# An S4D mixer with a channel MLP: kernel tables through DRAM, table products on GpSimd, outer products as blocks of their own

## The chip, the core and the metric

The kernel runs on one core of a Trainium2 chip. The metric is the device time of one execution in microseconds (us), median of three runs. The engines are TensorE (PE; its weight loads are shown apart as PEld), VectorE (DVE), ScalarE (ACT), GpSimd (POOL) and SyncE (SP, which issues most transfers).

## What is computed

The reference, cut to what matters (L = 2048 tokens, D = 576 channels, N = 128 states, F = 4608):

```python
xn = layernorm(A_u)
# s: a long convolution per channel, whose kernel K is made from the parameters
dt = exp(log_dt);  A = -exp(log_A_real) + 1j * A_imag;  C = (C_real + 1j * C_imag) * dt
P = exp((A * dt)[:, :, None] * arange(L))          # D x N x L
K = 2 * einsum("dn,dnl->dl", C, P).real
s = causal_conv(xn, K) + xn * D_skip               # by FFT
# g: an MLP over the channels of each token
h = gelu(layernorm(xn) @ w1 + b1)
g = silu(h @ w2 + b2)
out = A_u + s * g
```

## The kernel before

**The MLP is the frame.** 48 slots run one after the other: 12 groups of 384 hidden units, twice (two halves of the tokens), for two blocks of 512 tokens each. A slot is three products of layer 1 (line 633; 14 matmuls into a bank `mxa` or `mxb`, float32 split into a high and a low part, so that each product is done three times) and eight pieces of layer 2 (line 707; 72 matmuls of 288 columns). Between the two stand, for each of the three products, a GELU (ACT, 671), its high part `hh` (ACT, 674) and its low part `hl` (DVE, 677). DVE adds layer 2 to `acc` (717). ACT and DVE also split each weight tile, `raw`, into two parts (586, 583). Where the program finds it possible, the small last matmuls of two layer-1 products of the next slot are done ahead as a pair of half-height matmuls (`pair`, line 616); the two products then have 13 matmuls and not 14.

**The convolution is laid between.** The convolution kernel is made from 36 tables of 16 channels (`tables`, from line 953). For a table, `load_par` (944) fetches 16 channels' parameters from DRAM to `par` on POOL's queue; DVE multiplies angle and time into a phase (963, `w<-par,tv`) and adds a start (966); ACT and DVE cut it to its fraction and fold it (969, 972, 975), ACT takes two sines (980, 982); DVE multiplies powers into magnitudes `mg` (988, two instructions) and weighs the sines with them (997 to 1003). Then `kgen` does the outer products on PE (line 1042), a block of 64 small matmuls into a bank `cv`, and ACT copies it to `kt` in SBUF (1047). Six chunks of 96 channels (`chunk`, from line 1076) take these, with `xn`, through an FFT made of matmuls: 12 blocks `x1` (1157), 12 blocks `k1` (1188), 24 blocks `s2` (1217), 12 inverse blocks (1260) and 6 blocks `i1` (1286), with copies, transposes and products on ACT and DVE between them.

**What sets the order.** A planner (class `Order`) writes the order of each engine's instructions. It keeps a clock for each engine from fixed costs (`dve(n)`, `act(n)`, `pool(n)`), takes the steps of each line of work when its clock says that what they need is ready, and pins the result: each engine runs its instructions in that order. Steps of GELU and `hl` are urgent; others are put where they fit in ahead of these by the planner's clock. A block of the convolution is placed on PE when the planner's clock says that its input has been ready for 0.4 us (`pe_turns`, 1584). For the outer products there are two ways. `ride` (1053) puts them into another convolution block, so that PE goes from the MLP to both and back once. Otherwise `pe_turns` places them alone, after a patience `ALONE` of 20 us and not ahead of a date `DUE`. `HOLD` (1074) puts eight single steps behind the next instruction or two of their engine.

In DRAM stand among others `par_s` (the parameters of all channels), `xn_s`, `s_s` (the convolution's result), and `f2q`, `g2p` (the FFT's matrices, loaded as `f2t` and `g2t` on SP's queue, 1097 and 1100).

Of the kernel before, what the change touches and what calls it, by code (L numbers as in the profile page):

```python
# [28 lines left out]
E1, E8, E64, E512 = 2, 10, 18, 26  # L29
NPAR = 30  # L30
PK = 144
NXC, NROW = 1, 4
# [15 lines left out]
def pool(n):  # L48
    return 0.25 + 0.0023 * n

# [174 lines left out]
def mixer_kernel(ctx, tc, u, log_a_real, a_imag, c_real, c_imag, log_dt, d_skip, w1, b1, w2, b2,  # L225
# [24 lines left out]
    par_s = dr.tile([P, D, NPAR], F32, name="par_s")  # L250

# [13 lines left out]
    f1t = sb.tile([P, 2, 2, 64], F32, name="f1t")  # L265
# [34 lines left out]
    def odd_rows(part):  # L300
# [14 lines left out]
        if part == 1:  # L315
            for g in range(4):
                r = slice(32 * g, 32 * g + 32)
                V.tensor_copy(f1t[r, g % 2], bc(e[r], 1, 2))
                V.tensor_copy(f1t[r, 1 - g % 2].rearrange("p a b -> p (a b)"), o[r])
            return  # L320
# [82 lines left out]
    def norms(b0, n):  # L403
# [49 lines left out]
        def second(t):  # L453
            mv, rs = MV[b0]
            y = sb.tile([P, D], F32, name="row", bufs=NROW)
# [333 lines left out]
    def finish(b, c0, c1, silu, second_queue, z=None, store=(0, 0), flush=False,  # L789
# [7 lines left out]
        def act_z():  # L797
            if n < D:
                T.append(sb.tile([P, TB], F32, name="h32", bufs=2)[:, :n])
            else:  # L800
                T.append(sb.tile([P, D], F32, name="row", bufs=NROW))
# [33 lines left out]
    def params():  # L835
# [9 lines left out]
        PRM = [flat(sb.tile([P, 12, 64], F32, name="kt", bufs=2)) for _ in range(2)]  # L845
# [57 lines left out]
        add("DVE", d, lambda: V.scalar_tensor_tensor(cr, cr, 2.0, dt, op0=OP.mult, op1=OP.mult), mark="polar")  # L903
        early.append(step("DVE", d, lambda: V.tensor_mul(nrm, nrm, dt), need=["nrm"]))
# [5 lines left out]
        def pack(i):  # L910
            s = slice(i * PK, (i + 1) * PK)

            def columns():
                if i == 0:
                    V.memset(pt[:, :, E1:E1 + 17:8], 1.0)
                V.tensor_copy(pt[:, :, 0], th[:, s])
                V.tensor_copy(pt[:, :, 1], ph[:, s])
# [11 lines left out]
            early.append(step("DVE", 0.6 if i else 1.1, columns, need=["polar"]))  # L929
# [7 lines left out]
    PAR, TAB = {}, {}  # L937

    def load_par(b):
        if b == NB:  # L940
            return
        PAR[b] = sb.tile([P, SB, NPAR], F32, name="par", bufs=2)

        nc.gpsimd.dma_start(PAR[b].rearrange("p (g i) k -> p g (i k)", g=4), dram(  # L944
            par_s, (b // 3 * 48 + b % 3 * 4) * NPAR, [[D * NPAR, P], [12 * NPAR, 4], [1, 4 * NPAR]]))

    def bc(ap, dim, n):

        a = [list(x) for x in ap.ap]
        a.insert(dim, [0, n])  # L950
        return bass.AP(tensor=ap.tensor, offset=ap.offset, ap=a)

    def tables(b):
# [5 lines left out]
        def phase(k):  # L959
            if k == 0:  # L960
                T["v"] = table_tile()
                T["w"] = T["v"][:, :, :, 32:]
                nc.vector.tensor_mul(T["w"][:, 1], bc(PAR[b][:, :, 0], 2, NV), bc(tv, 1, SB))
            else:
                u = T["w"][:, 1, :, 33:]
                nc.vector.tensor_add(u, u, bc(PAR[b][:, :, 1], 2, 32))

        def whole():
            nc.scalar.activation(T["w"][:, 0].bitcast(I32), T["w"][:, 1], AF.Copy)

        def frac():
            nc.vector.tensor_sub(T["w"][:, 1], T["w"][:, 1], T["w"][:, 0].bitcast(I32))
# [11 lines left out]
        def mags(k):  # L984
# [3 lines left out]
            nc.vector.tensor_mul(T["m"][:, :, 64 * k:64 * k + 8 * n].rearrange("p c (i j) -> p c i j", i=n),  # L988
                                 bc(PAR[b][:, :, e8:e8 + n], 3, 8), bc(PAR[b][:, :, e1:e1 + 8], 2, n))

        def weigh(part):
# [10 lines left out]
            else:  # L1002
# [5 lines left out]
        return ([step(None, 10.0 if b < 6 else 4.5, lambda: load_par(b), mark=("par", b), need=[("pack", b * SB // PK)]  # L1008
                      + ([("mags", b - 2)] if b > 1 else [("xn", k) for k in range(8, NT)])),
                 step("DVE", dve(SB * NV), f(phase, 0), need=[("kg", b - 2)] if b > 1 else []),  # L1010
                 step("DVE", dve(n), f(phase, 1), hold=HOLD.get(("phase", b), 0)), step("ACT", act(SB * NV), whole),
                 step("DVE", dve(SB * NV), frac, hold=HOLD.get(("frac", b), 0)), step("ACT", act(SB * NV), fold, mark=("fold", b))],
                [step("ACT", act(SB * NV), f(sin, 0), need=[("fold", b)], mark=("sin", b, 0), tbl="sin"),
                 step("ACT", act(SB * NV), f(sin, 1), mark=("sin", b, 1), tbl="sin")],
                [step("DVE", dve(2 * n), f(mags, 0), need=[("par", b)]),
                 step("DVE", dve(n), f(mags, 1), mark=("mags", b))]
                + [step("DVE", dve((2, 2, 1, 1)[part] * n), f(weigh, part), need=[("sin", b, 1)],
                        mark=("wu", b) if part == 3 else None, hold=HOLD.get(("weigh", b, part), 0)) for part in range(4)])

# [9 lines left out]
    def kgen(b):  # L1029
# [3 lines left out]
        def mm(tile=None):  # L1033
            U, v = TAB[b]
            if r % 48 == 0:
                KT[c, r // 48] = sb.tile([P, 12, 64], F32, name="kt", bufs=2)
# [9 lines left out]
        def out():  # L1046
            nc.scalar.activation(KT[c, r // 48][:, k0:k0 + SB // 4, :].rearrange("p (h i) m -> p h (i m)", h=2),
                                 Q[0], AF.Copy)
        need = [("kp", c - 1, r // 48)] if r % 48 == 0 and c else []
# [24 lines left out]
    HOLD = {("weigh", 19, 3): 1, ("phase", 19): 1, ("frac", 18): 2, ("k", 2, 1): (2, 1), (2, 0, 24): 1, (2, 1, 24): 1, ("k1", 2, 1, 2): 1}  # L1074

    def chunk(c):

        XC, MAT, YS = {}, {}, {}
        one, two, three, four = [], [], [], []
# [23 lines left out]
        FP, PARTS2 = {}, {}  # L1103

        def f1_parts():

            f = f1t.rearrange("p v f k -> p v (f k)")

            def high():
                FP[0] = sb.tile([P, 2, 2, 128], F32R, name="f2t")  # L1110
                nc.scalar.activation(FP[0][:, 0], f, AF.Copy)
# [705 lines left out]
```

## Time and profile before

| | |
|---|---|
| median of 3 runs | 1095.29 us (1095.28 to 1095.74) |
| the profiled execution: span | 1094.6 us |
| what lies around the span, by the median | 0.7 us |
| PE busy in it | 1087.5 us, 11445 matmuls |
| DVE, ACT, POOL busy | 891.6, 727.4, 188.3 us |
| transfers | 138.22 MB, mean 126 GB/s |

The span is from the first to the last instruction. A row of a group view gives line, engine, operation, what is written and read, count, busy time, mean, and then the idle time of the engine just before, with what ended it. A row of the chain gives start, duration and work: its pieces lie end to end, so that a piece's duration holds the gap ahead of it. In the view of waits the three numbers are the total, the count and the longest.

### The profile page before, as it was taken

How to read it: one execution, taken by the hardware profiler on the slowest of the kernel's cores; microseconds unless marked ns; L12 is line 12 of the kernel's file. 1: busy time of each engine (PE TensorE's matmuls, PEld its weight loads, DVE VectorE, ACT ScalarE, POOL GpSimd, SP SyncE). 2: the span in 40 equal slices, each digit the busy share in tenths (PEclk: the TensorE clock that was granted, in tenths of full speed). 3: DMA queues.
4: the chain of work that ended last, by engine and by line, in shares of the span. 5: the costliest groups of instructions: out<-in, count | busy, mean ns of one | idle time of the engine just before them, and what ended most of it. 6: DMA issues, size and time to landing. Idle time of an engine off the chain costs nothing.

```text
span 1094.6 us, 27052 instructions
## 1 busy us (share of the span) xinstructions
PE 1087.5 (99%) x11445; PEld 954.1 (87%) x11445; DVE 891.6 (81%) x1302; ACT 727.4 (66%) x1113; POOL 188.3 (17%) x261
## 2 busy tenths in 40 slices
PE   9999999999999999999999999999999999999998
PEld 7989899899888898888988888888888888888897
DVE  7698667889998879889899987997979888766367
ACT  6585699778676674777767848685675757534333
POOL 4566210153010100001100000000001021101132
PEclk9999999999999999999999999999999999999999
DMA  8846663626354152355624216133152434455454
GB/s 226 241 141 160 227 240 137 181 78 156 120 161 139 44 112 66 91 111 147 166 47 119 78 56 141 34 122 87 54 126 44 143 101 132 116 168 151 136 151 102
DMA packets 139554, 138.22 MB, mean 126 GB/s; under 512 B 88953, under 2 KB 105017, under 8 KB 138857
## 3 DMA queue, kind: packets, MB, share of 16 engines
q1 hardware_dynamic: 124424, 85.05, 29.4%
q0 software_dynamic: 14528, 50.71, 15.1%
q8 instruction: 89, 1.46, 0.6%
q10 hardware_dynamic: 480, 0.74, 0.3%
q14 instruction: 33, 0.26, 0.1%
HBM read 102.17 MB, written 36.63 MB: 127 GB/s over the span
## 4 chain that ended last, share of the span: by engine, by line
PE 95%; DMA 2%; DVE 1%; SPq 1%; issue 0%; ACT 0%; DVEq 0%
PE mxb L707 20%; PE mxa L707 20%; PE mxa L633 20%; PE mxb L633 20%; PE cv L1042 3%; PE cv L1217 3%; PE cv L1260 2%; PE cv L1286 2%; PE cv L1188 1%; PE cv L1157 1%; SPq L856 1%; DMA w<-in_A_u_dram 1%; DMA acc<-in_A_u_dram 0%; DMA h<-in_B_b_dram 0%; DVE st L423 0%; DMA raw<-in_B_w_dram 0%
## 5 line engine op out<-in xcount | busy, mean ns | idle before, releaser
L677 DVE TENSOR_TENSOR hl<-h,hh 128x512 fp32r<-128x512 f32 x144 | 98.4, 686 | 96.4 <-ACT hh L674 95.4
L707 PE MATMUL mxa<-w2h,hh 128*128 128x288 f32 x573 | 170.3, 297 | 0.0
L707 PE MATMUL mxb<-w2h,hh 128*128 128x288 f32 x573 | 170.2, 297 | 0.0
L707 PE MATMUL mxb<-w2h,hl 128*128 128x288 f32 x573 | 169.3, 296 | 0.2 <-DVE hl L677 0.2
L707 PE MATMUL mxa<-w2h,hl 128*128 128x288 f32 x573 | 169.1, 295 | 0.0
L707 PE MATMUL mxa<-w2l,hh 128*128 128x288 f32 x573 | 168.6, 294 | 0.0
L707 PE MATMUL mxb<-w2l,hh 128*128 128x288 f32 x573 | 168.6, 294 | 0.0
L671 ACT ACTIVATE h<-mxa,b1t 128x512 f32<-128x512 f32 x73 | 50.0, 687 | 99.2 <-PE mxa L633 97.8
L707 PEld LDWEIGHTS mxa<-w2h,hh 128*128 128x128 f32 x573 | 107.6, 188 | 5.9 <-issue 3.0
L707 PEld LDWEIGHTS mxb<-w2h,hh 128*128 128x128 f32 x573 | 107.6, 188 | 4.3 <-issue 1.7
L707 PEld LDWEIGHTS mxb<-w2l,hh 128*128 128x128 f32 x573 | 107.6, 188 | 0.8
L707 PEld LDWEIGHTS mxa<-w2l,hh 128*128 128x128 f32 x573 | 107.6, 188 | 0.6
L707 PEld LDWEIGHTS mxb<-w2h,hl 128*128 128x128 f32 x573 | 107.5, 188 | 0.5 <-DVE hl L677 0.4
L707 PEld LDWEIGHTS mxa<-w2h,hl 128*128 128x128 f32 x573 | 107.5, 188 | 0.0
L671 ACT ACTIVATE h<-mxb,b1t 128x512 f32<-128x512 f32 x71 | 48.8, 687 | 68.6 <-PE mxb L633 66.2
L674 ACT ACTIVATE hh<-h 128x512 fp32r<-128x512 f32 x144 | 90.7, 631 | 3.7
L944 POOL DMA_DIRECT2D par<-par_s x36 | 27.8, 773 | 367.8 <-DVE mg L988 324.8
L717 DVE TENSOR_TENSOR acc<-mxa,acc 128x576 f32<-128x576 f32 x87 | 65.4, 752 | 26.4 <-PE mxa L707 26.1
L717 DVE TENSOR_TENSOR acc<-mxb,acc 128x576 f32<-128x576 f32 (+1 forms) x89 | 65.8, 741 | 17.8 <-PE mxb L707 17.6
L633 PE MATMUL mxa<-XH,w1h 128*128 128x512 f32 x284 | 79.4, 401 | 0.0
L633 PE MATMUL mxb<-XH,w1h 128*128 128x512 f32 x280 | 77.6, 399 | 0.0
L633 PE MATMUL mxa<-XL,w1h 128*128 128x512 f32 x284 | 76.2, 390 | 0.0
(277 smaller groups left out, 2494.0 us busy)
## 6 DMA issues: line engine op xcount, KB each, us to landing
raw<-in_B_w_dram SPq DMA_DIRECT2D x72, 288.0 KB, 3.4
raw<-in_B_w_dram SPq DMA_DIRECT2D x96, 192.0 KB, 3.6
par_s<-A POOLq DMA_DIRECT2D x4, 2160.0 KB, 8.1
par<-par_s POOLq DMA_DIRECT2D x36, 240.0 KB, 3.7
f2t<-f2q SPq DMA_DIRECT2D x24, 256.0 KB, 3.7
g2t<-g2p SPq DMA_DIRECT2D x24, 256.0 KB, 4.3
bias<-XR SPq DMA_DIRECT2D x42, 128.0 KB, 3.6
raw<-in_B_w_dram SPq DMA_DIRECT2D x48, 96.0 KB, 3.8
```

Of the source, the lines that this page charges most:

```text
L633: nc.tensor.matmul(q, a, b, start=j == 0 and i not in BEGUN, stop=j == len(ops) - 1, skip_group_check=True)
L671: nc.scalar.activation(t, q, AF.Gelu_apprx_tanh, bias=b1t[:, k:k + 1], scale=1.0)
L674: LAST[0] = nc.scalar.activation(hh[:, i], t, AF.Copy)
L677: nc.vector.tensor_sub(hl[:, i], t, hh[:, i].bitcast(F32))
L707: nc.tensor.matmul(q[:, dh, :288], a[:, i, c], b[:, i, d], start=i == 0 and k == 0 and alone != 1, stop=i == G - 1 and k == 2, skip_group_ ...
L717: nc.vector.tensor_add(o, q[:, dh:dh + n, :288], b)
L856: nc.sync.dma_start(r[32 * g:32 * g + 32].rearrange("c (b n) -> c b n", n=32), dram(src[k], 32 * g, [[N, 32], [32 * N, D // 32], [1, 32]]))
L944: nc.gpsimd.dma_start(PAR[b].rearrange("p (g i) k -> p g (i k)", g=4), dram(par_s, (b // 3 * 48 + b % 3 * 4) * NPAR, [[D * NPAR, P], [12 * ...
L1042: nc.tensor.matmul(q[32 * g:32 * g + 32, i // 2, i % 2 * 64:i % 2 * 64 + 64], U[:, ri, 4 * g + i, :], v[:, ri, 4 * g + i, :], start=ri == ...
L1217: nc.tensor.matmul(Q[i][32 * q:32 * q + 32, f, ri::2], m[r, 4 * i + q, 32 * ri:32 * ri + 32], A2[r, 4 * p + 2 * i + q // 2, :, :, q % 2], ...
L1260: nc.tensor.matmul(QI[q // 2][64 * f:64 * f + 64, q % 2, i], MAT["g2t", p + i // 2][r, i % 2, f, ri], YS[p + i // 2][0][r, i % 2, ri, f], ...
L1286: nc.tensor.matmul(Q[h][64 * y:64 * y + 64, t], g1t.rearrange("p a e -> p (a e)"), A2[:, k:k + 2, 1].rearrange("p i d r -> p i r d"), star ...
```

## The change

- **Phases and magnitudes.** The two phase instructions and the two magnitude instructions of each table go from DVE to GpSimd (lines 987, 990 and 1014 of the changed kernel). The phase has its own tile `pb` (one buffer), its angle and start a small tile `pa`, loaded from a new DRAM tensor `turn_s`. `par` has one buffer where it had two, 28 columns where it had 30, and is loaded on SP's queue where it was loaded on POOL's. Lines of steps are split accordingly, with the planner's cost `gps(n)`.
- **Tables through DRAM.** ACT copies an outer product to a small tile `ko`, SP stores it to a DRAM tensor `kt_s`, and a chunk fetches 12 x 64 columns of it to `kl`. The tables no longer wait for a chunk to free `kt`.
- **Outer products alone.** `ALONE` is 0, the dates `DUE` are gone. `ride` is unchanged. The lines of the tables stand ahead of those of the chunks in the planner's list.
- **A shorter chain in a chunk.** The first matrix of the FFT, `fp`, is made once where it was made for each of the six chunks (1111, 1114 before). The copy that turned `xc` to `xt` ahead of its splitting (ACT, 1124) is gone: ACT and DVE now read `xc` in turned order themselves. The splitting of `x` and of `k` stand in lines of their own, the copies ahead of the FFT's products too (`six`).
- `HOLD` is empty, `END` (to which the planner paces the chunks) 990 and not 1000, `NROW` 3 and not 4.

The core of the diff:

```diff
-E1, E8, E64, E512 = 2, 10, 18, 26
-NPAR = 30
+E1, E8, E64, E512 = 0, 8, 16, 24
+NPAR = 28
...
+    def load_pa(b):
+        PA[b] = sb.tile([P, 2, SB], F32, name="pa", bufs=2)
+        nc.sync.dma_start(PA[b].rearrange("p v (g i) -> p v g i", g=4), dram(
+            turn_s, b // 3 * 48 + b % 3 * 4, [[2 * D, P], [D, 2], [12, 4], [1, 4]]))
...
-        PAR[b] = sb.tile([P, SB, NPAR], F32, name="par", bufs=2)
-        nc.gpsimd.dma_start(PAR[b].rearrange("p (g i) k -> p g (i k)", g=4), dram(
+        PAR[b] = sb.tile([P, SB, NPAR], F32, name="par")
+        nc.sync.dma_start(PAR[b].rearrange("p (g i) k -> p g (i k)", g=4), dram(
...
-                nc.vector.tensor_mul(T["w"][:, 1], bc(PAR[b][:, :, 0], 2, NV), bc(tv, 1, SB))
+                T["p"] = sb.tile([P, SB, NV], F32, name="pb")
+                nc.gpsimd.tensor_mul(T["p"], bc(PA[b][:, 0], 2, NV), bc(tv, 1, SB))
...
-                nc.vector.tensor_add(u, u, bc(PAR[b][:, :, 1], 2, 32))
+                nc.gpsimd.tensor_add(u, u, bc(PA[b][:, 1], 2, 32))
...
-            nc.vector.tensor_mul(T["m"][:, :, 64 * k:64 * k + 8 * n].rearrange("p c (i j) -> p c i j", i=n),
+            nc.gpsimd.tensor_mul(T["m"][:, :, 64 * k:64 * k + 8 * n].rearrange("p c (i j) -> p c i j", i=n),
...
-            nc.scalar.activation(KT[c, r // 48][:, k0:k0 + SB // 4, :].rearrange("p (h i) m -> p h (i m)", h=2),
-                                 Q[0], AF.Copy)
+            t = sb.tile([P, SB // 4, 64], F32, name="ko")
+            nc.scalar.activation(t.rearrange("p (h i) m -> p h (i m)", h=2), Q[0], AF.Copy)
+            nc.sync.dma_start(kt_s[b // 3, :, k0:k0 + SB // 4, :], t)
...
-            if which == "x":
-                four.append(step("ACT", act(2000), turn, need=need))
...
-    END = 1000.0
+    END = 990.0
...
-    ALONE, DUE = 20.0, (160.0, 950.0)
+    ALONE = 0
...
-                    wait = ("wu", b + 1) not in od.marks or od.t["PE"] < DUE[0] + b * (DUE[1] - DUE[0]) / NB
-                    if b < NB - 1 and od.t["PE"] < h[1] + (ALONE if wait else 3.0):
+                    if b < NB - 1 and od.t["PE"] < h[1] + ALONE:
```

What this does to the order of PE's instructions. Before, in the first chunk, behind a product of layer 1 (`mxb`): the outer products (`cv<-w`) stand right ahead of a block `s2` (`cv<-A_83,f2t`), with layer 1 on both sides of the two.

```order
L633 MATMUL mxb<-XH,w1l 128x512 x4
L633 MATMUL mxb<-XR,w1r 128x512
L633 MATMUL mxb<-XR,w1s 128x512
L1042 MATMUL cv<-w 32x64 x32
L1217 MATMUL cv<-A_83,f2t 32x2x96 x32
L633 MATMUL mxa<-XH,w1h 128x512 x4
L633 MATMUL mxa<-XL,w1h 128x512 x4
```

The changed kernel, at the first block `s2` of the same chunk (layer 1 is line 642 here, the outer products 1067, `s2` 1238):

```order
L642 MATMUL mxb<-XH,w1l 128x512 x4
L642 MATMUL mxb<-XR,w1r 128x512
L642 MATMUL mxb<-XR,w1s 128x512
L1067 MATMUL cv<-w 32x64 x32
L642 MATMUL mxa<-XH,w1h 128x512 x4
L642 MATMUL mxa<-XL,w1h 128x512 x4
L642 MATMUL mxa<-XH,w1l 128x512 x4
L642 MATMUL mxa<-XR,w1r 128x512
L642 MATMUL mxa<-XR,w1s 128x512
L1238 MATMUL cv<-A_85,f2t 32x2x96 x32
L642 MATMUL mxb<-XH,w1h 128x512 x4
```

Between the outer products and `s2` there is now a product of layer 1: PE leaves the MLP twice where it left it once. In the whole order 28 of the 36 blocks of outer products stood beside another block of the convolution before (8 alone), and 5 do now (31 alone). PE leaves the MLP for the convolution 77 times before and 100 times now. Of the pairs of line 616 there were 16, and there are 9; right ahead of a block `x1` stood 5, and stands 1. The first outer products stand behind 7 slots of the MLP (8 before), the last behind 30 of the 48 (41 before).

On DVE, before, in the stretch of a table: magnitudes (988) and phase (963, 966) stand with the three `hl` of a slot.

```order
L1003 SCALAR_TENSOR_TENSOR w<-w,mg 128x16x32
L988 TENSOR_TENSOR mg<-par 128x16x64
L988 TENSOR_TENSOR mg<-par 128x16x32
L677 TENSOR_TENSOR hl<-h_1903,hh 128x512
L677 TENSOR_TENSOR hl<-h_1941,hh 128x512
L963 TENSOR_TENSOR w<-par,tv 128x16x65
L966 TENSOR_TENSOR w<-w,par 128x16x32
L677 TENSOR_TENSOR hl<-h_2001,hh 128x512
```

On POOL in the changed kernel, in the first chunk: the phase (987, 990) and the magnitudes (1014) stand between issues of transfers (`g2p`, one of the FFT's matrices, put in order in DRAM).

```order
L987 TENSOR_TENSOR pb<-pa,tv 128x1040
L990 TENSOR_TENSOR pb<-pb,pa 128x16x32
L341 DMA g2p<-in_g_dram 256x1x32 x4
L1014 TENSOR_TENSOR mg<-par 128x16x64
L1014 TENSOR_TENSOR mg<-par 128x16x32
L987 TENSOR_TENSOR pb<-pa,tv 128x1040
L990 TENSOR_TENSOR pb<-pb,pa 128x16x32
```

The four instructions of a table have moved from DVE's order to POOL's; ACT's cut to a fraction now waits for POOL's phase, and DVE's weighing for POOL's magnitudes.

On SP, in the changed kernel's first chunk, the new transfers stand among the weight tiles (`raw`):

```order
L560 DMA raw<-in_B_w_dram 128x576 x2
L1074 DMA kt_s<-ko 128x256
L958 DMA par<-par_s 128x4x112
L560 DMA raw<-in_B_w_dram 128x576
L952 DMA pa<-turn_s 128x8x4
L562 DMA raw<-in_B_w_dram 128x384 x4
```

SP's queue has 36 stores to `kt_s`, 36 loads of `par`, 36 of `pa` and 12 of `kl` that were not on it before.

157 lines of the change are left out of this document (86 added, 71 removed).

## The prediction

> **What bounds the kernel now.** I read the head of the page first, then the chain that ended last and what PE waited for.
>
> ```profile
> PE 1087.5 (99%) x11445; PEld 954.1 (87%) x11445; DVE 891.6 (81%) x1302; ACT 727.4 (66%) x1113; POOL 188.3 (17%) x261
> PE 95%; DMA 2%; DVE 1%; SPq 1%; issue 0%; ACT 0%; DVEq 0%
> PE mxa L1348 <- POOL XL L1341: 1.3, 1, 1.3
> PE mxa L648 <- ACT XH L520: 0.4, 1, 0.4
> PE mxb L707 <- DVE hl L677: 0.2, 1, 0.2
> ```
>
> PE is busy for 99% of the span and makes 95% of the chain. All that the profile counts as its waits is 1.9 us in three waits, two of them on the first product's data. So DVE's 81% is no bound: what a change takes from DVE or ACT cannot come back as time unless PE's own row gets shorter. The question is what the change does to the length of PE's row, and whether it makes PE wait.
>
> PE's row has a price that no count of matmuls shows. In the chain, pieces lie end to end, so a piece's duration holds the gap ahead of it. First a block of outer products that stands alone between products of layer 1, then one that rides ahead of a block `s2`, then blocks `x1` with a pair (L616) ahead and without:
>
> ```profile
> 172.15 3.17 PE mxa L633 x14
> 175.32 1.03 PE cv L1042 x64
> 176.35 3.40 PE mxb L633 x14
> 179.75 1.58 PE mxa L707 x12
> ...
> 297.32 0.43 PE mxb L616 x2
> 297.75 1.59 PE cv L1217 x55
> 299.34 3.18 PE mxb L633 x13
> ...
> 308.63 1.03 PE cv L1042 x64
> 309.67 1.55 PE cv L1217 x59
> 311.22 1.79 PE mxa L707 x12
> ...
> 251.84 1.05 PE cv L1157 x11
> 269.37 1.25 PE cv L1157 x12
> ```
>
> A product of layer 1 takes 3.17 us, but 3.40 when PE comes back from the convolution to it: 0.23 more. Twelve matmuls of layer 2 take 1.58, and 1.79 on coming back: 0.21. I take 0.22 for one return. The outer products take 1.03 either way, and `s2` takes about the same behind a rider (1.55) as without (1.59). So a rider saves one return, 0.22 us.
>
> **The change part by part.**
>
> *Outer products alone.* By the order, PE leaves the MLP 100 times and not 77. 23 returns at 0.22 us are 5.1 us, all on PE's row, with nothing to hide them. Pairs: on a return a product without its 14th matmul takes 3.18 and not 3.40, so a pair saves 2 x 0.22 = 0.44 and costs 0.43. Seven fewer pairs cost nothing, but for those ahead of `x1`: there the block takes 1.05 and not 1.25 us. Four fewer of these cost 4 x 0.20 = 0.8 us. Matmuls are otherwise the same in number and shape. Sum for PE's row: 5.9 us.
>
> *Phases and magnitudes on GpSimd.* What leaves DVE, and what GpSimd's own element-wise products took:
>
> ```profile
> L963 DVE TENSOR_TENSOR w<-par,tv 128x1040 f32<-128x1040 f32 x36 | 44.2, 1227 | 0.0
> L966 DVE TENSOR_TENSOR w<-w,par 128x512 f32<-128x512 f32 x36 | 24.8, 688 | 0.7
> L988 DVE TENSOR_TENSOR mg<-par 128x1024 f32<-128x1024 f32 x36 | 43.9, 1221 | 0.8
> L988 DVE TENSOR_TENSOR mg<-par 128x512 f32<-128x512 f32 x36 | 24.6, 683 | 0.0
> L583 POOL TENSOR_TENSOR w1l<-raw,w1h 128x384 fp32r<-128x384 f32 x2 | 2.0, 1008 | 0.1
> L820 POOL TENSOR_TENSOR w<-w,A 128x576 f32<-128x576 f32 x1 | 1.4, 1449 | 2.8 <-PE mxa L707 2.8
> ```
>
> DVE loses 44.2 + 24.8 + 43.9 + 24.6 = 137.5 us. Worth nothing directly, as DVE is not the bound. On POOL 192 elements more cost 1449 - 1008 = 441 ns, 2.3 ns each, and 0.13 us are fixed. So 1040, 512, 1024 and 512 elements take 2.5, 1.3, 2.5 and 1.3 us: 7.6 us per table, 274 us for 36. POOL has 188.3 us now, so it does not become the bound. But the tables are done between slots 7 and 30, and 23 slots of 1094.6/48 = 22.8 us are 524 us: in them POOL multiplies for 52% of the time.
>
> Does that disturb DVE? Where it matters is the third `hl` of a slot, for which PE has no cushion: the matmul that needs it starts as soon as it is there.
>
> ```profile
> 568.07 0.68 DVE L677 TENSOR_TENSOR hl<-h,hh 128x512 fp32r<-128x512 f32 x1
> 568.83 0.37 PE L707 MATMUL mxb<-w2h,hl 128*128 128x288 f32 x1
> ```
>
> `hl` ends at 568.75 and its matmul starts at 568.83, drawn out from 0.29 to 0.37. Each slot has one such place; a DVE instruction that is late there is late on PE. How DVE fares beside GpSimd shows in the normalization, at the start:
>
> ```profile
> 84.42 0.69 DVE L677 TENSOR_TENSOR hl<-h,hh 128x512 fp32r<-128x512 f32 x1 [1.93 <-ACT hh L674]
> 85.03 1.02 DVE L583 TENSOR_TENSOR w1l<-raw,w1h 128x384 fp32r<-128x384 f32 x2
> 86.87 1.46 DVE L583 TENSOR_TENSOR w1l<-raw,w1h 128x384 fp32r<-128x384 f32 x2
> ...
> 83.40 2.29 POOL L466 TENSOR_SCALAR w<-w,mv,rs 128x576 f32<-128x576 f32 x1
> 86.63 2.29 POOL L466 TENSOR_SCALAR w<-w,mv,rs 128x576 f32<-128x576 f32 x1
> ...
> 57.16 3.97 POOL L466 TENSOR_SCALAR w<-w,mv,rs 128x576 f32<-128x576 f32 x1 [11.07 <-ACT w2h L586]
> 56.89 2.09 DVE L583 TENSOR_TENSOR w2l<-raw,w2h 128x576 fp32r<-128x576 f32 x3
> 58.90 1.22 DVE L876 TENSOR_TENSOR kt<-kt,pr 128x576 f32<-128x576 f32 x1
> ```
>
> Inside POOL's 2.29 us instruction an `hl` takes its usual 0.69. Two `w1l` take 1.02 at one time and 1.46 at another. Of the nine DVE instructions in these rows two are drawn out, by some 0.45 us each (1.46 against 1.02; 1.22 against 2.09 / 3 = 0.70 for the same 576 elements), and POOL's own went from 2.29 to 3.97. That is 0.1 us for each DVE instruction that meets one of POOL's: 23 places x 0.52 x 0.1 = 1.2 us. These POOL instructions have one tensor input, the new ones two, so the price may be several times that.
>
> The Trainium skill speaks against this part more strongly. Its page "SBUF — State Buffer", section "Who interferes with whom", says that a DVE instruction with two SBUF inputs and a GpSimd instruction that reads SBUF exclude each other, and that the second to issue is blocked until the first has finished. The `hl` above, which reads two tiles, was not blocked; the 3.97 us fit the rule better. I keep it as a rival.
>
> *Waits for GpSimd.* ACT's cut (`whole`) waits for the phase, with the next GELU queued behind it; DVE's weighing waits for the magnitudes, with `hl` and `acc` behind it; PE's outer products wait for the weighing, with the MLP behind them. The planner places these by its clock with 0.4 us to spare, and `ALONE` = 0 takes away the 20 us of patience that outer products had. The same 0.4 us are the rule for the other blocks of the convolution, 66 of them, and PE's waits above have none on their inputs: the planner's clock is good where DVE and ACT are concerned. For POOL nothing shows it. Bounds: nothing, or 31 blocks late by half a microsecond, 15 us. A gain is excluded, as no wait on a table is there to remove. `HOLD` is empty too. I take 1.6 us, near the lower end, since the nearest rows (the 66 blocks) are at nothing.
>
> *SP's queue.* `par`, `pa`, `kt_s` and `kl` now stand in SP's queue, behind weight tiles and matrices that wait:
>
> ```profile
> SPq L1097 <- PE cv L1217: 86.9, 18, 8.2
> ```
>
> A `par` behind an `f2t` can start 8.2 us late. Its cover: it is asked for when the table before has its magnitudes, and used when that one's weighing is done and POOL has multiplied; at 36 tables in 524 us, 14.6 us each, less the 7.6 us of POOL, that is an estimated 5 us or more. I cost it at nothing; without the cover it is a rival. The stores and loads of `kt` add about 10 MB to 138.22, hidden by the slack of tables that end 11 slots earlier than before.
>
> *The chunk's chain.* The turning copy (ACT) goes, while splitting in turned order costs more:
>
> ```profile
> L1124 ACT ACTIVATE xt<-xc 128x768 f32<-128x768 f32 x12 | 25.2, 2099 | 0.2 <-DMA xc<-xn_s 0.2
> ```
>
> ACT loses 12 copies of 2.1 us and gets back up to as much, since its first splitting now reads in turned order; so does DVE's. That is 25.2 us on engines that are 66% and 81% busy, beside PE: nothing. Made once, `fp` saves both a little. The start and the last chunk's end don't change the row either: the final 12 us hang on the MLP's last additions, not on the convolution.
>
> **The sum.** The profiled span is 1094.6 us, 0.7 below the median of 1095.29. 1095.3 + 5.9 (PE's row) + 1.2 (DVE beside POOL) + 1.6 (late blocks) = 1104.0 us.
>
> **The rivals.**
>
> *The exclusive lock.* If a DVE instruction with two SBUF inputs waits for the end of POOL's, it meets on average (2.5² + 1.3² + 2.5² + 1.3²) / (2 x 7.6) = 1.0 us of rest. 23 x 0.52 x 1.0 = 12 us in place of 1.2: about 1115 us. For: the 3.97 us, the 1.46. Against: seven of nine instructions undisturbed. Chance 0.13. The rule of the "SBUF" page of the Trainium skill would give this.
>
> *The wait moves to the parameters.* If each chunk's `f2t` waits hold back a `par` beyond its cover, weighing is late and `hl` behind it: 6 chunks x some 3 us = 18 us, about 1119 us. For: the 8.2 us, POOL's in-order queue, in which phases stand between magnitudes. Against: the cover. It decides from a delay of about 5 us on. Chance 0.13.
>
> *The return is cheaper, and the kernel not slower.* If the 0.22 us hang on how busy DVE and ACT are, they shrink with DVE's 137.5 us. The kernel before pays 77 x 0.22 = 16.9 us, the changed one 100 x p + 0.8: from p = 0.16 down it is no slower; at half the price it takes 1095.3 - 16.9 + 11 + 0.8 + 2.8 = 1093 us. Against: the gap is the same wherever I look, and no row has PE wait on an engine after the start. Chance 0.05.
>
> *The placing changes nothing.* Were part of PE's row slack that the profile counts as busy, 23 returns could be free: 1095 us. Against: the pieces above. Chance 0.03.
>
> **How the numbers follow.** The forecast, PE's row with a few us of waits (1100.5 to 1108), has 0.66: 1104.0 us. The range reaches from PE's row alone with the start's waits gone, 1099.5, over the lock's case, to 1116; the parameters' case and the two cheap ones are left out in part. A difference of 0.2% (2.2 us) is about what can be told from no change. Slower 0.92 (forecast, lock, parameters), same 0.03, faster 0.05.
>
> **What would show it.** Right: PE's chain has 3.4 us pieces of layer 1 behind single pieces of 1.03 us, about 100 returns at 0.22; PE is still busy for 98% or more; its waits name DVE's `hl`, ACT's GELU or the weighing, for a few us in all. The lock: DVE's mean for `hl` well over 690 ns, PE's waits on it over 10 us. The parameters: DVE waits on POOL's `mg`, POOL on transfers of `par`. I am wrong if a return costs other than 0.2 us, or if the start or the end moves by more than a microsecond.

## The result, and the profile after

The changed kernel takes 1158.36 us (median of 4 runs, 1156.77 to 1159.73) where the kernel before takes 1095.34: a ratio of 1.0577 (1.0562 to 1.0592). It is slower, as forecast, but by 63 us and not by 9, and outside the forecast's range, which ended at 1116. The profiled execution took 1156.77 us and its span is 1154.9, 60.3 more than before.

The head of the page, the chain by engine, and what PE waited for (total, count, longest), in the changed kernel:

```profile
PE 1112.0 (96%) x11445; PEld 962.8 (83%) x11445; DVE 889.9 (77%) x1145; ACT 692.3 (60%) x1077; POOL 417.7 (36%) x369
PE 64%; DVE 23%; issue 4%; ACT 4%; DMA 2%; SPq 1%; POOL 0%; DVEq 0%; ACTq 0%; POOLq 0%
PE mxa L716 <- DVE hl L686: 9.5, 9, 2.7
PE mxb L716 <- DVE acc L726: 7.8, 5, 2.1
PE mxb L716 <- DVE hl L686: 5.7, 6, 2.6
```

PE's share of the chain fell from 95% to 64% and DVE's rose from 1% to 23%, although four instructions per table had left DVE. DVE was busy 891.6 us before and 889.9 now: 137.5 us went and nearly as much came back. DVE's groups show where it came back (count, busy time, mean ns of one, idle time ahead):

```profile
L686 DVE TENSOR_TENSOR hl<-h,hh 128x512 fp32r<-128x512 f32 x144 | 135.6, 947 | 139.2 <-ACT hh L683 139.1
L726 DVE TENSOR_TENSOR acc<-mxa,acc 128x576 f32<-128x576 f32 x87 | 65.2, 749 | 38.7 <-PE mxa L716 38.4
L1025 DVE TENSOR_TENSOR w<-w,mg 128x1024 f32<-128x1024 f32 x36 | 55.5, 1540 | 0.0
L1023 DVE TENSOR_TENSOR w<-w,mg 128x1024 f32<-128x1024 f32 x36 | 50.2, 1393 | 3.0 <-ACT w L1008 1.5 <-POOL mg L1014 1.4
```

The same groups in the kernel before:

```profile
L677 DVE TENSOR_TENSOR hl<-h,hh 128x512 fp32r<-128x512 f32 x144 | 98.4, 686 | 96.4 <-ACT hh L674 95.4
L717 DVE TENSOR_TENSOR acc<-mxa,acc 128x576 f32<-128x576 f32 x87 | 65.4, 752 | 26.4 <-PE mxa L707 26.1
L997 DVE TENSOR_TENSOR w<-w,mg 128x1024 f32<-128x1024 f32 x36 | 43.9, 1218 | 4.0 <-ACT w L982 4.0
L999 DVE TENSOR_TENSOR w<-w,mg 128x1024 f32<-128x1024 f32 x36 | 43.8, 1218 | 0.0
```

`hl` took 686 ns before and takes 947; the weigh steps (997, 999 before) took 1218 and take 1393 and 1540. Both read two tiles in SBUF. `acc`, which reads one operand from a bank, took 752 and takes 749. So DVE is not slower as such: its instructions with two inputs in SBUF are.

One place shows how this reaches PE. The changed kernel in order of time, DVE, then POOL, then PE (start, duration, work):

```profile
485.09 2.97 DVE L1023 TENSOR_TENSOR w<-w,mg 128x1024 f32<-128x1024 f32 x1
487.99 2.08 DVE L1025 TENSOR_TENSOR w<-w,mg 128x1024 f32<-128x1024 f32 x1
489.99 0.68 DVE L1027 TENSOR_TENSOR w<-w,mg 128x512 f32<-128x512 f32 x1
490.60 0.68 DVE L1029 SCALAR_TENSOR_TENSOR w<-w,mg 128x512 f32<-128x512 f32 x1
491.20 0.68 DVE L686 TENSOR_TENSOR hl<-h,hh 128x512 fp32r<-128x512 f32 x1
...
484.64 2.34 POOL L987 TENSOR_TENSOR pb<-pa,tv 128x1040 f32<-128x1040 f32 x1 [3.42 <-DVE w L998]
487.06 1.92 POOL L990 TENSOR_TENSOR pb<-pb,pa 128x512 f32<-128x512 f32 x1
...
488.79 0.30 PE L716 MATMUL mxa<-w2h,hh 128*128 128x288 f32 x1
488.92 0.29 PE L716 MATMUL mxa<-w2l,hh 128*128 128x288 f32 x1
491.93 0.61 PE L716 MATMUL mxa<-w2h,hl 128*128 128x288 f32 x1 [2.72 <-DVE hl L686]
492.34 0.44 PE L716 MATMUL mxa<-w2h,hh 128*128 128x288 f32 x1
492.58 0.44 PE L716 MATMUL mxa<-w2l,hh 128*128 128x288 f32 x1
```

POOL's phase runs to 486.98, its start addition to 488.98. DVE's weigh step beside the first ends at 488.06, the one beside the second at 490.07: each 1.1 us after POOL's end, about what it takes alone (1.2). It looks as if neither advanced while POOL worked. POOL's addition was held too: it took 1.92 us here and 1.06 at its shortest. The two short steps and the `hl` behind them take their usual 0.68, but start 2.6 us late, and PE stands for 2.72 us. Behind that its matmuls start 0.24 us apart and not 0.13; the last section comes back to this.

The 144 `hl`, laid beside POOL's phases and magnitudes one by one, show a rule. 48 of them overlap with such an instruction in time. 39 began after it: 38 of these ended 0.54 to 0.63 us after its end, however long that took, and the other one ran into the next of POOL's instructions and ended 0.56 us after that. The nine that began before POOL's instruction took their usual 0.68 to 0.69 us, and POOL's instruction took 2.28 to 2.38 where it takes 1.95 alone. So of an `hl` and such an instruction, whichever begins second waits for the end of the first.

Three things in the forecast were as told: outer products alone with a return to layer 1 behind them, as in the chain of the changed kernel,

```profile
154.94 1.03 PE cv L1067 x64
155.97 3.40 PE mxb L642 x14
159.37 3.17 PE mxa L642 x14
```

a start and an end that did not move (1.3 us ahead of PE's first instruction in both, 5.5 behind its last and 5.2 before), and no loss through `par` (POOL waits 8.8 us in all for it to land, DVE 1.4 us for `mg`). One sign was not as told: PE is busy for 96% of the span and not for 98% or more.

For all that follows I split each profiled span into five parts: the 1.3 us ahead of PE's first instruction; PE's idle time between its first and last instruction; half the time at clock 0.50 ahead of the last matmul; what lies behind PE's last instruction; and the rest, which is PE's row itself. Idle time within half clock stands in both columns, so that PE's row is too short by 2.4 us in run 8, by 2.0 in run 1 and by at most 1.6 elsewhere.

| run | median us | span | PE idle | half clock | PE's row | behind |
|---|---|---|---|---|---|---|
| before | 1095.3 | 1094.6 | 0.6 | 0 | 1087.5 | 5.2 |
| changed | 1158.4 | 1154.9 | 36.1 | 10.2 | 1101.8 | 5.5 |
| 1 products on DVE | 1127.3 | 1126.1 | 15.9 | 8.5 | 1091.1 | 9.3 |
| 2 chunks' lines first | 1146.6 | 1145.7 | 29.4 | 6.8 | 1099.4 | 8.8 |
| 3 before, alone | 1124.3 | 1121.6 | 9.1 | 3.4 | 1091.0 | 16.8 |
| 4 changed, riding | 1135.9 | 1129.6 | 23.6 | 5.1 | 1094.3 | 5.3 |
| 5 one input | 1121.3 | 1119.1 | 14.6 | 1.7 | 1096.0 | 5.5 |
| 6 fills | 1111.7 | 1112.4 | 8.0 | 3.4 | 1094.1 | 5.5 |
| 7 before, no `HOLD` | 1097.4 | 1094.7 | 1.3 | 0 | 1086.9 | 5.1 |
| 8 before, products on POOL | 1153.5 | 1153.4 | 39.2 | 17.1 | 1090.2 | 5.6 |
| 9 fills, riding | 1112.0 | 1108.2 | 10.5 | 3.4 | 1087.6 | 5.3 |
| 10 on DVE, riding | 1120.3 | 1118.9 | 15.7 | 5.1 | 1087.6 | 9.0 |
| 11 planner 1.3 | 1130.6 | 1132.0 | 21.3 | 5.1 | 1099.0 | 5.3 |
| 12 stalls | 1125.8 | 1123.9 | 19.6 | 6.8 | 1091.0 | 5.2 |
| 13 as 9, row in time | 1102.8 | 1100.4 | 4.7 | 0 | 1089.0 | 5.4 |
| 14 as 10, in time | 1103.4 | 1102.4 | 4.0 | 0 | 1088.0 | 9.0 |
| 15 planned, riding | 1138.2 | 1136.5 | 24.1 | 6.8 | 1094.8 | 9.4 |

The changed kernel's 60.3 us are 35.5 of idle time, 10.2 of half clock, 14.3 in PE's row and 0.3 at the end.

### The profile page after: what moved, and what is told of

Read it like the earlier page. It is cut to its first block, busy times and chain, and to the rows that moved or that the text cites. A ratio compares the mean times of both kernels' runs of the same rounds, so it can differ in the third digit from the quotient of the medians.

```text
span 1154.9 us, 27320 instructions
## 1 busy us (share of the span) xinstructions
PE 1112.0 (96%) x11445; PEld 962.8 (83%) x11445; DVE 889.9 (77%) x1145; ACT 692.3 (60%) x1077; POOL 417.7 (36%) x369
## 4 chain that ended last, share of the span: by engine, by line
PE 64%; DVE 23%; issue 4%; ACT 4%; DMA 2%; SPq 1%; POOL 0%; DVEq 0%; ACTq 0%; POOLq 0%
PE mxb L716 14%; PE mxa L716 13%; PE mxb L642 13%; PE mxa L642 13%; DVE hl L686 3%; PE cv L1238 3%; DVE w L1025 2%; DVE acc L726 2%; DVE w2l L592 2%; DVE w L1027 2%; DVE w L998 2%; DVE w L1023 2%; PE cv L1067 2%; PE cv L1284 2%; DVE w1l L592 2%
## 5 line engine op out<-in xcount | busy, mean ns | idle before, releaser
L686 DVE TENSOR_TENSOR hl<-h,hh 128x512 fp32r<-128x512 f32 x144 | 135.6, 947 | 139.2 <-ACT hh L683 139.1
L716 PE MATMUL mxb<-w2h,hh 128*128 128x288 f32 x573 | 174.1, 304 | 7.9 <-DVE acc L726 7.8
L716 PE MATMUL mxb<-w2h,hl 128*128 128x288 f32 x573 | 172.0, 300 | 5.9 <-DVE hl L686 5.7
L1014 POOL TENSOR_TENSOR mg<-par 128x1024 f32<-128x1024 f32 x72 | 123.5, 1736 | 102.0 <-DVE w L1029 90.5
L987 POOL TENSOR_TENSOR pb<-pa,tv 128x1040 f32<-128x1040 f32 x36 | 81.1, 2252 | 142.4 <-DVE w L998 142.2
L767 POOL DMA_DIRECT2D out_dram<-row x32 | 17.1, 540 | 193.0 <-DVE row L764 178.2
```

The source lines that it names most:

```text
L686: nc.vector.tensor_sub(hl[:, i], t, hh[:, i].bitcast(F32))
L716: nc.tensor.matmul(q[:, dh, :288], a[:, i, c], b[:, i, d], start=i == 0 and k == 0 and alone != 1, stop=i == G - 1 and k == 2, skip_group_ ...
L987: nc.gpsimd.tensor_mul(T["p"], bc(PA[b][:, 0], 2, NV), bc(tv, 1, SB))
L1014: nc.gpsimd.tensor_mul(T["m"][:, :, 64 * k:64 * k + 8 * n].rearrange("p c (i j) -> p c i j", i=n), bc(PAR[b][:, :, e8:e8 + n], 3, 8), bc(P ...
```

## The experiments

My first theory behind the result was the forecast's rival, the lock: DVE stands while POOL reads. The other theory was placing: outer products alone, the tables ahead of the chunks and an empty `HOLD` make PE's inputs late whoever multiplies.

**1. Products back on DVE.** The changed kernel; the planner's steps for the products go to DVE with them, and the chunks' lines go ahead of the tables'.

```diff
-                nc.gpsimd.tensor_mul(T["p"], bc(PA[b][:, 0], 2, NV), bc(tv, 1, SB))
+                nc.vector.tensor_mul(T["p"], bc(PA[b][:, 0], 2, NV), bc(tv, 1, SB))
...
-                nc.gpsimd.tensor_add(u, u, bc(PA[b][:, 1], 2, 32))
+                nc.vector.tensor_add(u, u, bc(PA[b][:, 1], 2, 32))
...
-            nc.gpsimd.tensor_mul(T["m"][:, :, 64 * k:64 * k + 8 * n].rearrange("p c (i j) -> p c i j", i=n),
+            nc.vector.tensor_mul(T["m"][:, :, 64 * k:64 * k + 8 * n].rearrange("p c (i j) -> p c i j", i=n),
```

> The changed kernel with the phases and the magnitude products back on VectorE; so that the planner finds room for them, the chunks' lines stand ahead of the tables' lines. All else of the change stays (tables through DRAM, outer products mostly alone: 16 more returns than before). Exclusion (a VectorE instruction with two SBUF inputs and a GpSimd product with two SBUF inputs keep each other out): the mean of hl falls from 947 to below 700 ns, PE's waits from 37 to below 6 us, no stretch at half clock, 1098 to 1104 us. Placing (outer products alone and tables early leave PE no cushion, whichever engine multiplies): 1135 us or more.

1127.31 us (ratio 1.0268, 1.0223 to 1.0312); `hl` 686 ns. Neither theory's number. DVE's `hl` is free again, but DVE stood once for 10.19 us in front of a tile from DRAM, PE for 7.2 of it, with 6.8 us at half clock behind it, and as much behind a second such wait (`kl`, 5.6 us, PE 3.9):

```profile
116.07 0.69 DVE L686 TENSOR_TENSOR hl<-h,hh 128x512 fp32r<-128x512 f32 x1 [3.82 <-ACT hh L683]
126.96 1.24 DVE L987 TENSOR_TENSOR pb<-pa,tv 128x1040 f32<-128x1040 f32 x1 [10.19 <-DMA pa<-turn_s]
128.12 0.68 DVE L686 TENSOR_TENSOR hl<-h,hh 128x512 fp32r<-128x512 f32 x1
```

The `hl` that PE needed was ready to run and stood behind the phase in DVE's order. So there is a third cause that neither theory had: an instruction in an engine's fixed order whose data is still on its way from DRAM.

**2. The lines' order alone.** The changed kernel with that one line of the planner's list.

```diff
-... xl, wx, kl, sl, tl, vl, ol, al, rl, phl, c3, c2, c6, c1, c5, c4, kfl, gl, odl, fl = ...
+... xl, wx, c3, c2, c6, c1, c5, c4, kfl, kl, sl, tl, vl, ol, al, rl, phl, gl, odl, fl = ...
```

> The changed kernel with only the order of the planner's lines changed as in the run with the products on VectorE; the products stay on GpSimd. It tells whether that order made the difference there. Exclusion: hl stays near 930 ns, 1140 to 1165 us. If the order of the lines is what matters: below 1115 us.

1146.61 us (1.0464, 1.0449 to 1.048), `hl` 898 ns. 12 us of run 1's gain were this line's; the products' move made the rest, 19 us, with run 1's two late tiles counted against it.

**3. Outer products alone, in the kernel before** (the lines that used `DUE` go too).

```diff
-    HOLD = {("weigh", 19, 3): 1, ...
+    HOLD = {}
...
-    ALONE, DUE = 20.0, (160.0, 950.0)
+    ALONE = 0
```

> The kernel before with only the rule for outer products changed (ALONE 0, no dates) and HOLD empty: 26 blocks alone, 18 more returns. Exclusion, with the ledger of returns: 1095.3 + 18 x 0.22 = 1099.3, and up to 3 us of small waits, 1099 to 1103 us. Placing: more than 1115 us.

1124.34 us (1.0262, 1.0246 to 1.0277), with `hl` at 687: a miss by over 20 us. The returns are as forecast, PE's row is 3.5 us longer. The rest is two accidents. At 479 SP's queue held a row's load behind an `f2t` that had waited 8.3 us for PE; DVE's transposition of that row then held `acc`, and PE stood 5.1 us, with 6.8 us at half clock behind it. DVE, then SP:

```profile
483.88 0.71 DVE L491 STREAM_TRANSPOSE row<-row 128x512 f32<-128x512 f32 x1 [4.55 <-DMA row<-y_s]
486.00 0.71 DVE L491 STREAM_TRANSPOSE row<-row 128x512 f32<-128x512 f32 x1 [1.40 <-DMA row<-y_s]
...
478.86 0.32 SPq L1097 DMA_DIRECT2D f2t<-f2q  x1
479.23 7.29 SPq L486 DMA_DIRECT2D row<-y_s  x12
```

And the last chunk's output was fetched so late that DVE waited 7.0 us for it behind PE's last matmul: 16.8 us there and not 5.2.

**4. The changed kernel with the outer products riding again.**

```diff
-    ALONE = 0
+    ALONE, DUE = 20.0, (160.0, 950.0)
...
-                    if b < NB - 1 and od.t["PE"] < h[1] + ALONE:
+                    wait = ("wu", b + 1) not in od.marks or od.t["PE"] < DUE[0] + b * (DUE[1] - DUE[0]) / NB
+                    if b < NB - 1 and od.t["PE"] < h[1] + (ALONE if wait else 3.0):
```

> The changed kernel with the old rule for outer products (patience 20 us and dates): 7 alone, as many returns as before. Exclusion: only the 24 returns come back, about 5 us, and the blocked instructions stay: 1143 to 1156 us, hl near 930 ns. Placing: below 1115 us.

1135.94 us (1.0358, 1.0336 to 1.038), `hl` 894. In the profiled execution (1131.4 us) PE's row is 7.5 us shorter, its idle time 12.5. That is more than the returns that I expected back. Either the placing counts for more while DVE is held, or this order happens to fit better; run 11 moves the time as much by another order, so the two are not told apart.

**5 and 6. The same order, with GpSimd reading less.** These leave the changed kernel's order as it is, every POOL instruction at its place. Run 5 gives it one input and leaves the second factor out. Run 6 gives it none: it leaves the phases and products out and makes three fills of the same output.

```diff
-                nc.gpsimd.tensor_mul(T["p"], bc(PA[b][:, 0], 2, NV), bc(tv, 1, SB))
+                nc.gpsimd.tensor_scalar(T["p"], bc(PA[b][:, 0], 2, NV), 0.5, None, op0=OP.mult)
```

```diff
-                nc.gpsimd.tensor_mul(T["p"], bc(PA[b][:, 0], 2, NV), bc(tv, 1, SB))
+                [nc.gpsimd.memset(T["p"], 0.25) for _ in range(3)]
```

(and so for the other two lines.)

> The changed kernel in its own order, every phase and product instruction on GpSimd kept in place and size but reading one tensor instead of two (it multiplies by a constant, so the second factor is left out and the outputs are others). If what the changed kernel lost is VectorE held by GpSimd's two-input instructions, the third-part writes hl fall from 947 ns back to under 740, the large two-input weigh steps from 1540 and 1393 back to under 1300, TensorE's waits from 37 us to under 15, the half-clock windows go, and the time is 1105 to 1125 us. If it is the placing of the outer products and the order of the work, which this run leaves as it is, the time stays at 1145 to 1160 us and TensorE still waits over 25 us.

> The changed kernel in its own order, every phase and product instruction on GpSimd replaced by three fills of the same output with a constant: GpSimd writes and reads nothing (phases and products are left out, the outputs are others). If the holding comes from GpSimd's reading, VectorE is undisturbed: hl under 740 ns, 1105 to 1125 us as with one input. If any GpSimd access to the memory holds VectorE, hl stays over 850 ns and the time over 1140 us.

1121.33 us (1.0242, 1.0225 to 1.0259) and 1111.72 us (1.0152, 1.0134 to 1.017). DVE's `hl` and one POOL group, with one input:

```profile
L686 DVE TENSOR_TENSOR hl<-h,hh 128x512 fp32r<-128x512 f32 x144 | 107.4, 749 | 160.6 <-ACT hh L683 160.3
L1014 POOL TENSOR_SCALAR mg<-par 128x1024 f32<-128x1024 f32 x72 | 158.7, 2222 | 48.8 <-DVE w L1029 45.5
```

With fills:

```profile
L686 DVE TENSOR_TENSOR hl<-h,hh 128x512 fp32r<-128x512 f32 x144 | 98.9, 689 | 173.8 <-ACT hh L683 173.8
L1014 POOL MEMSET mg<- 128x1024 f32 (+1 forms) x216 | 158.1, 742 | 52.9 <-DVE w L1028 44.6
```

With one input `hl` stayed a little above the 740 ns that I had expected. Together the two runs settle it: order, matmuls and transfers are the same, POOL is busy longer than in the changed kernel (479.8 us against 417.7), and 46.6 of the 63 us are gone with its reads. (Fills do not wait for `pa` or `par` either; but run 5's instructions do, and 37 of the 63 us are gone there.) Of the 144 `hl`, those that ran beside one of POOL's new instructions, by the trace: in the changed kernel 48, of which 35 took over 750 ns, the 48 on average 1467; with one input 57, 21 over 750, on average 843; with fills 61, none over 750, on average 689. Those beside none took 687 or 688 in all three. The Trainium skill has the rule, on its page "SBUF — State Buffer", section "Who interferes with whom": a DVE instruction with two SBUF inputs contends with a GpSimd instruction that reads SBUF, and not with one that only writes it. The fills bear out its second half to a nanosecond, the weigh steps above the first. One input held DVE much less than two, though those instructions were longer (2222 ns against 1736); the rule makes no such difference. In run 5 most `hl` that began inside one of POOL's instructions ended before it did; why it is so stays open.

**7. `HOLD` emptied, nothing else,** in the kernel before.

```diff
-    HOLD = {("weigh", 19, 3): 1, ("phase", 19): 1, ("frac", 18): 2, ("k", 2, 1): (2, 1), (2, 0, 24): 1, (2, 1, 24): 1, ("k1", 2, 1, 2): 1}
+    HOLD = {}
```

> The kernel before with its table of held-back steps emptied and nothing else. The forecast took the table at nothing: 1094 to 1098 us. If the steps that it held back now stand in an engine's order ahead of data that a transfer still brings, as the transposes of a row did in the run with the outer products alone (VectorE idle 4.6 us, TensorE 5.1 us, then 6.8 us at half clock), one or two such waits cost 5 to 12 us each: 1100 to 1120 us, with the waits on VectorE put down to a DMA.

1097.38 us (1.0018, 1.0008 to 1.0028). The table is worth 2 us; run 3's accidents are not its.

**8. The products on POOL, nothing else** of the change in the kernel before but the empty `HOLD`. (`END`, the planner's pace for the chunks, is 850 here, neither the 1000 of before nor the 990 of the changed kernel.)

```diff
-                nc.vector.tensor_mul(T["w"][:, 1], bc(PAR[b][:, :, 0], 2, NV), bc(tv, 1, SB))
+                nc.gpsimd.tensor_mul(T["w"][:, 1], bc(PAR[b][:, :, 0], 2, NV), bc(tv, 1, SB))
...
-                nc.vector.tensor_add(u, u, bc(PAR[b][:, :, 1], 2, 32))
+                nc.gpsimd.tensor_add(u, u, bc(PAR[b][:, :, 1], 2, 32))
...
-            nc.vector.tensor_mul(T["m"][:, :, 64 * k:64 * k + 8 * n].rearrange("p c (i j) -> p c i j", i=n),
+            nc.gpsimd.tensor_mul(T["m"][:, :, 64 * k:64 * k + 8 * n].rearrange("p c (i j) -> p c i j", i=n),
```

> The kernel before with its phases and products on GpSimd and nothing else of the change but the emptied table of held-back steps; outer products still ride with others and tables are made as before. If VectorE is held by GpSimd: hl over 850 ns, weigh steps stretched as in the changed kernel, TensorE waits 15 to 35 us, 1115 to 1145 us. If the loss sat in the outer products' placing and the tables' way through DRAM: 1090 to 1103 us with hl near 690.

1153.5 us (1.0535, 1.052 to 1.0551), above even the lock's expectation. `hl` and PE's longest wait:

```profile
L681 DVE TENSOR_TENSOR hl<-h,hh 128x512 fp32r<-128x512 f32 x144 | 132.3, 922 | 155.6 <-ACT hh L678 155.0
PE mxb L711 <- DVE acc L721: 15.2, 7, 4.5
```

PE's row is 1090.2, outer products ride: this one part alone brings a loss nearly as large as the whole change, though in an order of its own, so that the size is this order's.

**9. What is left without the lock: fills, and riding.** Run 6 with run 4's edit.

> The run with fills in place of GpSimd's phases and products (left out again, the outputs are others), and the rule for the outer products put back to that of before: they ride with other blocks where they can, PE leaves the MLP some 21 times less. What remains of the loss in the run with fills, 16.7 us, is then taken apart. If a return costs 0.22 us as forecast and the rest is late data, the time falls by 4 to 7 us, to 1105 to 1108 us. If placing the outer products alone costs more than its returns, because each lonely block stands where its input is late, it falls to 1095 to 1101 us.

1111.95 us (1.0149, 1.0133 to 1.0164), no gain over run 6, yet PE's row is back at 1087.6 us. The 6.5 us that it shortened are the 20-odd returns; they were eaten by one wait, the row of run 3 again, in which PE stands 5.5 us with 6.8 us at half clock behind it:

```profile
481.76 1.02 DVE L592 TENSOR_TENSOR w1l<-raw,w1h 128x384 fp32r<-128x384 f32 x2
488.76 0.71 DVE L500 STREAM_TRANSPOSE row<-row 128x512 f32<-128x512 f32 x1 [5.98 <-DMA row<-y_s]
```

**10. Products on DVE, riding:** run 1 with run 4's edit.

> The changed kernel with phases and products back on VectorE, the chunks' lines ahead of the tables' and the outer products riding again; tables through DRAM, the single fp and the shorter chain stay. If nothing is lost but VectorE held by GpSimd, the lonely returns and accidental waits on transfers: 1095 to 1101 us when no transfer is late, 1105 to 1120 us when VectorE again stands for 5 us or more ahead of a tile from DRAM as it did in the run with the products on VectorE. If the tables' way through DRAM costs by itself, TensorE waits on many small places and the time is over 1105 us without one long wait.

1120.3 us (1.0223, 1.0206 to 1.024). PE's row 1087.6 again, and the two late tiles again: DVE waits 10.5 us for `pa` and 4.2 for the row.

**11. A planner that knows that DVE is slower beside GpSimd.**

```diff
-            dur *= 1.1
+            dur *= 1.3
```

> The changed kernel, its planner told that VectorE's instructions take 1.3 times their cost beside GpSimd's and not 1.1 times. If the loss is that the planner puts work closer than the held VectorE can do it, the order spreads out and the time falls by 8 us or more, to 1135 to 1150 us. If an instruction is held by whatever of GpSimd's stands beside it, between nothing and 2 us, a mean factor doesn't help: 1152 to 1165 us.

1130.61 us (1.0327, 1.0311 to 1.0343): 28 us less, though `hl` still takes 894 ns.

**12. Stalls made on purpose,** in the kernel before: ACT copies the third GELU of twelve slots onto itself 2 to 5 times.

```diff
+    STALL = {8: 2, 10: 2, 12: 2, 14: 3, 16: 3, 18: 3, 20: 4, 22: 4, 24: 4, 28: 5, 30: 5, 32: 5}
...
+            for _ in range(STALL.get(now, 0) if i == G - 1 else 0):
+                nc.scalar.activation(t, t, AF.Copy)
```

> The kernel before with twelve slots of the MLP in which ACT copies the third GELU onto itself 2, 3, 4 or 5 times more, 0.63 us each, so that TensorE stands still for about 1.3, 1.9, 2.5 and 3.2 us, three times each, with nothing of GpSimd beside it. If half clock follows from TensorE's own idle time (over half of a stretch of 3.413 us, as in the runs so far), none follows the 1.3 us stalls, one follows some of the 1.9 us ones and most of the 2.5 and 3.2 us ones, unless a stall lies across two stretches: 26 us of waits and 8 to 18 us of half clock, 1125 to 1140 us. If half clock came with GpSimd's work or its contention, there is none here: 1119 to 1124 us.

1125.76 us in one run. PE stood less than meant (0.4, 1.05, 1.35 to 2.3, and 2.4 us: the GELU had some 0.8 us to spare), and half clock followed in four places, each behind a stretch with over 2.2 us of idle time. Two stretches around the first of them; the columns are the stretch, its length, the busy time of PE, PEld, DVE, ACT and POOL with the count, the granted clock, the share of DMA and GB/s:

```profile
439.81:443.22 3.41, 1.11 (x9) 0.88 (x7) 3.41 (x6) 0.15 (x1) 0.00 (x0) 1.00 0.71 197
443.22:446.64 3.42, 3.42 (x15) 3.42 (x16) 2.27 (x3) 1.08 (x1) 0.75 (x1) 0.50 0.17 63
```

POOL does nothing in the first stretch. So half clock follows from PE's own idling, whatever the reason.

**13 to 15. The late tiles in time.** The planner gave a row's load 6.5 us, counted from the last work of its line, which was long past; now from when it is asked for. Run 13 is run 9 with that, run 14 run 10 with that and 20 us for the first `pa` (4.5 before). Run 15 is run 4 with it and a factor of 1.2.

```diff
-            ml["steps"].append(step(None, 6.5, load, need=at("t", kb - 1) + at("l", kb - 2), mark=M("s", kb)))
+            ml["steps"].append(step(None, 6.5, load, at=0.0 if tb or kb else od.t["PE"] + 6.5, need=at("t", kb - 1) + at("l", kb - 2), mark=M("s", kb)))
```

> The run with fills and riding outer products (GpSimd's phases and products left out), with the planner told that the first row's load from DRAM begins when it is asked for and not long before, so that VectorE's transposition of that row stands some 12 us further back. If the 6.0 us wait of VectorE, the 7.7 us of waits of TensorE behind it and its half clock are all that was left of the loss, the time is 1096 to 1101 us. If another order only brings another wait of that kind, it stays at 1105 to 1112 us.

> The changed kernel with phases and products on VectorE and riding outer products, the first row's load timed as in the other run and the first table's angles counted 20 us for their way from DRAM and not 4.5 (they took 18.1 us). Without the two waits of VectorE (10.5 and 4.2 us) the tables through DRAM, the single fp and the shorter chain stand alone: 1096 to 1102 us if they cost nothing, and no gain over the kernel before, since TensorE's row is as long. Over 1105 us would mean that the tables' way through DRAM costs by itself.

> The changed kernel with phases and products on GpSimd as it has them, riding outer products, the first row's load timed as in the other run, and the planner's factor for VectorE beside GpSimd at 1.2 and not 1.1. If planning helps against a held VectorE as it did with 1.3 alone (28 us less), this comes to 1108 to 1122 us, still well over the kernel before. If the gain of 28 us was an accident of one order: 1126 to 1137 us, as with riding outer products alone.

Run 13: 1102.78 us (1.0063, 1.0048 to 1.0078); run 14: 1103.38 (1.007, 1.0055 to 1.0085). Nine and 17 us less than runs 9 and 10, no half clock, PE's row at 1089.0 and 1088.0; both a little above what I expected. Of run 14's 7.8 us over the kernel before, 3.8 are at the end (the last chunk's output now stands behind the last matmul) and 3.4 are idle time. So without the lock, the returns and the two late tiles, the rest of the change costs little and brings nothing; no version beat the kernel before. Run 15: 1138.17 (1.0391, 1.0372 to 1.041), no better than run 4. So run 11's 28 us were one order's luck, or hang on a factor of 1.3 with lonely outer products; what is shown is that no order tried with POOL's products in it (six, 1130.6 to 1158.4 us) came within 35 us.

## Why the prediction was wrong

- **Right:** that PE's row bounds the kernel and that DVE's relief is worth nothing. POOL's own time: forecast 274 us, measured 258. PE's row by returns: forecast 5.9 us, measured 6.6 (run 6, the same order without the lock, against before), and back at 1087.6 with riding. The shorter chain, the single `fp`, the tables through DRAM: forecast nothing, about nothing (run 14, but for its end). SP's queue and `par`: not the cause in the changed kernel.
- **The step that failed: "That is 0.1 us for each DVE instruction that meets one of POOL's: 23 places x 0.52 x 0.1 = 1.2 us."** Both factors failed. The price: an `hl` that meets POOL's product takes 1467 ns and not 687, 0.78 us more and not 0.1. The nine instructions that I took it from stood beside POOL's instructions with one tensor input, and run 5 shows that one input is another case (843 ns, 0.16 more). I had written that two might cost several times that, and yet took the measured tenth as the value. The count: not 23 third `hl` but every DVE instruction with two SBUF inputs, since DVE runs in order and what is held delays all behind it. DVE was busy 889.9 us with POOL reading and 781.6 with fills: 108 us of holding, some 37 of it on `hl`, 38 on the weighing and 17 on the low parts of the weights. Of the kernel's time it cost 46.6 us, in place of 1.2. (Not all that came back to DVE is holding: the splitting of `x` in turned order takes 24.5 us where it took 11.4.)
- **The rival had the mechanism and a wrong size.** The lock at 12 us, again for the third `hl` alone, set the range's end at 1116. The rule that it names is what the 48 `hl` show, and 0.78 us of waiting each is less than the 1.0 that it took; the count was too small. It cost 46.6. Between the profiles of the changed kernel and of run 6 (spans 42.5 apart) these are 28.1 us of idle time, 6.8 of half clock and 7.7 in PE's row (matmuls that start a little late without a gap that the trace shows as idle; this last reading is argued, not shown).
- **Late blocks: forecast 1.6 us;** run 6 has 7.4 us more idle time than before, and 3.4 of half clock, which no term had. The nearest rows were "at nothing" because that order happened to be so: in runs 1, 3, 9 and 10 a single tile from DRAM cost 5 to 11 us, its half clock with it.
- **`HOLD`: forecast nothing, 2 us.**

## What to carry to other kernels

Before moving elementwise work to GpSimd, count VectorE's instructions with two SBUF inputs that would run beside it: here 38 of the 39 `hl` that began inside a GpSimd product of two inputs ended just behind it, and in a fixed order everything behind waited too. A row of a similar operation with fewer operands is no bound for the price. When an order is made anew, look first for an engine's longest single wait for a transfer: one of 5 to 10 us can hide what the experiment was to show.

## What I had not expected of the hardware

The granted clock. It fell to 0.50 for whole stretches of 3.413 us, once PE had idled for about half of the stretch before. Three stretches of the changed kernel, with the columns as in run 12, the first holding the 2.72 us wait:

```profile
488.28:491.70 3.42, 0.93 (x8) 0.70 (x6) 3.42 (x4) 3.13 (x3) 1.05 (x2) 1.00 0.54 117
491.70:495.11 3.41, 3.18 (x13) 3.18 (x14) 3.41 (x5) 0.84 (x1) 3.41 (x3) 0.50 0.02 5
495.11:498.53 3.42, 3.42 (x83) 3.16 (x82) 2.93 (x5) 1.36 (x2) 0.18 (x1) 1.00 0.42 123
```

PE was busy for 0.93 of the first 3.42 us. In the 13 profiles that have half clock ahead of the last matmul I laid out the stretches at full clock with over 0.9 us of idle time: 53 with less than 1.55 us, none followed by half clock; 36 with 1.85 us or more, all followed by it; of 12 between, 4 were. So a wait of 2 us costs an estimated 3.7 (2 and half of 3.413) if it falls into one stretch, and 2 if it falls across two, as one of 2.56 us did in run 5. The Trainium skill's page "TensorE: Matmul & The Clock Gate", section "Part 1: The HAM clock gate (the "warmup" mystery)", speaks of a free-running window of 3413 ns, as here, and of an idle window ahead of half clock; by these runs half an idle one is enough.
